# Hash matmuls in two column halves, PSUM copies moved to ScalarE, a first head without DMAs between its operands, and a new order: one core of Trainium2

## The chip, the core and the metric

The kernel runs on one core of one Trainium2 chip. A core has TensorE (PE in the profile; its weight loads are shown as PEld), VectorE (DVE), ScalarE (ACT), GpSimd (POOL) and SyncE (SP, which only issues DMAs here). Matmul results land in PSUM, from where VectorE or ScalarE must copy them to SBUF. The metric is the device time of one execution in microseconds.

## The reference

Sixteen attention heads (batch 2, 8 heads, 768 positions, width 64) whose mask is a hash: a query sees a key only if the signs of their projections on 6 vectors agree. Then two layers over 1536 tokens of width 512 with 2048 hidden units each.

```python
q_bits = (np.einsum('bhsd,dk->bhsk', q, proj) > 0)
k_bits = (np.einsum('bhsd,dk->bhsk', k, proj) > 0)
...
mask = q_bucket[:, :, :, None] == k_bucket[:, :, None, :]
scores = scale * np.matmul(q, k.transpose(0, 1, 3, 2))
scores = np.where(mask, scores, -1000000000.0)
scores = scores - np.max(scores, axis=-1, keepdims=True)
attn = np.exp(scores)
attn = attn / (np.sum(attn, axis=-1, keepdims=True) + 1e-09)
return np.matmul(attn, v).astype(np.float32)
...
h = x @ w_in                                   # layer 0
g = np.maximum(h, 0.0) + np.log1p(np.exp(-np.abs(h)))
return (g @ w_out).astype(np.float32)
...
h = x @ w_in                                   # layer 1
relu6 = np.clip(h + 3.0, 0.0, 6.0)
g = h * relu6 / 6.0
return (g @ w_out).astype(np.float32)
```

The weights of the layers come as 64-bit floats.

## The kernel before

**No loop of the program sets the order of the work.** Every step is entered in a plan (`Schedule.add`) with its engine or engines, an assumed cost in microseconds, what it reads and writes, and a priority (a due time). `Schedule.run` (line 98) then plays the plan through with those costs: at each step it takes, on the unit that comes free first, the ready operation with the least due time, gives an operation that two engines may do to the one that ends it first, and writes it out. The emitted order on each engine is fixed and in order. So a change of a cost or of a due time (`TH`, `WHEN`, `STEP`, `PROJECT`, `ACTIVATE`, `FETCH`, `AHEAD`, lines 35 to 48) moves operations on all engines.

**A head** (`prepare`, line 279, and `attend`, line 375). Three loads bring `raw` (keys transposed in partitions 0 to 63, queries in 64 to 127, in two DMAs) and `rawk` (the keys twice). Scores are taken with split numbers: `qa` holds the rest and the rounded part of the queries, `ka` the rounded keys twice, `qb` the rounded queries again and `kb` the rest of the keys; rows 64 to 95 of `qb` and `kb` hold the hash bits, which add a large positive number where query and key agree. The bits come from the hash matmuls `dot` (line 339): `hashes` times `raw`, one matmul for each half of the 768 positions, both summed into all 128 rows of the PSUM tile `d`. A comparison on VectorE (L356) turns `d` into `bt`, and four DMAs (L365) send `bt` to the rows of `qb` and `kb`. One more DMA (L334) copies the rounded queries from `qa` to `qb`.

For each of 6 query tiles: four score matmuls into `sc` (L392, L393; two PSUM buffers), the row maximum (`nm`, L406, VectorE) and a bias (`bs`, L413, VectorE), the exponential (`e`, L421, ScalarE), six transposes into `tp` (L432, one PSUM buffer), and a copy of `tp` to `et` in SBUF (`even`, L436, by either engine). Per head: 12 value matmuls into `av` (L448; each pair writes rows 0 to 63 and 64 to 127 of the same tile; a matmul in full precision, as these and the hash matmuls are, shows as two rows of the trace), a copy to `xa` (by either engine), three transposes into `pt`, the reciprocal of the row sums (`rec`, two VectorE instructions, L474 and L478), and a scaled copy to `xn` (L485). Per two heads, transposes `xt` and a split into `xh` and `xl`.

**Layers.** Weights are loaded as 64-bit words and converted by seven operations per tile (`convert`: two on ScalarE, five on VectorE, all on tiles called `raw`, `bits`, `w`). Each layer has 32 tiles. The first 12 of layer 0 have room beside the attention; its other 20 wait until the attention's SBUF is free, and those of layer 1 until the tiles of layer 0 that lie in their place have had their last use, in the third group. Hidden matmuls `ph` (L605, 12 for each of 16 blocks in 3 groups of 512 tokens), then the activation, then projections into `acc` (L697 in layer 0, L699 in layer 1, 12 for each block). The activation of layer 0 goes ScalarE (`me`, `mu`, `ml`), VectorE (`me`, L665), GpSimd (`ml`, L672, shown as L231), VectorE (`ml`, L676), ScalarE (`gh`), VectorE (`gl`).

Copies, casts and subtractions are recorded at the lines of their helpers: L226 is a copy on ScalarE, L228 a copy on VectorE, L231 a subtraction on VectorE or GpSimd; the tile names tell them apart.

## Time and profile before

| | us |
|---|---|
| median of 3 runs (843.8 to 844.47) | 844.27 |
| the profiled execution's own time | 844.39 |
| its span, first to last instruction | 842.7 |
| TensorE busy | 799.3 (95%) |
| VectorE busy | 558.9 (66%) |
| ScalarE busy | 451.5 (54%) |
| GpSimd busy | 92.1 (11%) |

What lies outside the span is 1.7 us. The granted TensorE clock is 1.00 of full speed (2.4 GHz) in every stretch, which says nothing of matmuls at the very start: the first ones take about twice as long as later ones of their kind.

A row of the page's groups reads: line, engine, operation, output<-input, shapes, count | busy time, mean ns of one | idle time of the engine before them and what ended it. A row of the order of time reads: start, duration, engine, line, operation, and in brackets the idle time before it with its releaser. Durations overlap a little: an instruction often starts some 0.07 to 0.1 us before the one ahead of it has ended, so the distance of two starts is the cost on a full engine. A busy TensorE is not TensorE at its peak, since ends of matmuls are modelled. The program falls into an opening (no exponential yet), the sixteen heads, and the two layers.

### The profile page before, as it was taken

What the parts mean: (1) busy time and instruction counts of PE and PEld (TensorE: products, weight loads), DVE (VectorE), ACT (ScalarE), POOL (GpSimd) and SP (SyncE); (2) the same over time, 40 slices, a digit from 0 to 9 for tenths busy, and PEclk for the clock granted to TensorE, in tenths of its full rate; (3) what the DMA queues carried; (4) which work ended last, traced back from release to release, by engine and by line L of the source; (5) the groups of instructions that cost most, each with busy time, mean ns of one, the idle gap of its engine ahead of it and who ended that gap; (6) DMA issues with size and microseconds to landing.
All of it is one profiled execution on the core that took longest, in us unless ns stands there. A gap on an engine that the chain in (4) does not pass through costs nothing.

```text
span 842.7 us, 10395 instructions
## 1 busy us (share of the span) xinstructions
PE 799.3 (95%) x3808; PEld 604.5 (72%) x3808; DVE 558.9 (66%) x958; ACT 451.5 (54%) x764; POOL 92.1 (11%) x85
## 2 busy tenths in 40 slices
PE   4899999999999999999999999999999999999997
PEld 2666666666666667677888776677888888888886
DVE  4989999999887889964333698989942322232222
ACT  1677677777665767656554766775532322232222
POOL 1000000000000242322222224340000000000000
PEclk9999999999999999999999999999999999999999
DMA  7584323332310650000000255451000100010001
GB/s 191 166 271 103 82 80 93 86 85 75 86 29 28 254 228 0 1 1 1 0 1 1 93 157 167 158 175 50 1 1 1 50 1 1 0 51 1 1 0 51
DMA packets 26771, 59.40 MB, mean 70 GB/s; under 512 B 3680, under 2 KB 7776, under 8 KB 26720
## 3 DMA queue, kind: packets, MB, share of 16 engines
q1 hardware_dynamic: 24224, 52.45, 20.6%
q10 hardware_dynamic: 2496, 6.29, 2.1%
q8 instruction: 30, 0.49, 0.2%
q14 instruction: 21, 0.17, 0.1%
HBM read 49.29 MB, written 3.15 MB: 62 GB/s over the span
## 4 chain that ended last, share of the span: by engine, by line
PE 65%; DVE 16%; ACT 5%; DMA 5%; POOL 4%; issue 4%; SPq 1%; ACTq 0%; DVEq 0%; POOLq 0%
PE ph L605 22%; PE acc L699 16%; PE acc L697 7%; PE av L448 7%; PE tp L432 5%; POOL ml L231 4%; PE sc L392 4%; PE sc L393 3%; DVE gl L231 2%; DVE bits L576 2%; DVE bits L569 2%; PE d L340 2%; ACT e L421 2%; DMA raw<-in_moe_w_out_dram 2%; DVE me L665 2%
## 5 line engine op out<-in xcount | busy, mean ns | idle before, releaser
L605 PE MATMUL ph<-xh,w 128*128 128x512 f32 x768 | 240.8, 395 | 0.8 <-ACT xa L226 0.6
L605 PEld LDWEIGHTS ph<-xh,w 128*128 128x128 f32 x768 | 143.7, 188 | 34.5 <-ACT xa L226 1.3
L605 PE MATMUL ph<-xl,w 128*128 128x512 f32 x384 | 151.2, 394 | 0.0
L421 ACT ACTIVATE e<-sc,bs 128x768 f32<-128x768 f32 x96 | 95.0, 990 | 64.2 <-DVE bs L413 44.9
L634 DVE SCALAR_TENSOR_TENSOR ml<-me,ph 128x512 f32<-128x512 f32 x48 | 33.0, 687 | 124.6 <-ACT me L629 124.6
L697 PE MATMUL acc<-gh,w 128*128 128x512 f32 x384 | 101.0, 400 | 11.7 <-ACT gh L226 11.3
L231 POOL TENSOR_TENSOR ml<-ml,me 128x512 f32<-128x512 f32 x48 | 85.9, 1789 | 210.3 <-DVE me L665 154.2
L406 DVE TENSOR_REDUCE nm<-sc 128x1 f32<-128x768 f32 x96 | 91.7, 955 | 22.1 <-PE sc L393 20.6
L629 ACT ACTIVATE me<-ph,three 128x512 f32<-128x512 f32 x48 | 33.1, 689 | 133.7 <-PE ph L605 130.7
L699 PE MATMUL acc<-w,gh 128*128 128x512 f32 x384 | 97.8, 393 | 0.0
L697 PEld LDWEIGHTS acc<-gh,w 128*128 128x128 f32 x384 | 69.9, 188 | 37.2 <-ACT gh L226 22.7
L605 PEld LDWEIGHTS ph<-xl,w 128*128 128x128 f32 x384 | 72.1, 188 | 17.0
L699 PEld LDWEIGHTS acc<-w,gh 128*128 128x128 f32 x384 | 72.1, 188 | 16.7
L392 PE MATMUL sc<-ka,qa 128*128 128x384 f32 x192 | 76.7, 400 | 7.0 <-ACT e L421 6.6
L432 PE MATMUL tp<-ident,e 128*128 128x128 f32 x576 | 80.1, 275 | 3.2 <-DVE et L228 1.7
L432 PEld LDWEIGHTS tp<-ident,e 128*128 128x128 f32 x576 | 66.8, 140 | 16.0 <-ACT et L226 5.2
L448 PE MATMUL av<-et,vx 128*64 128x384 f32 x384 | 72.1, 498 | 0.0
L393 PE MATMUL sc<-kb,qb 96*128 96x384 f32 x192 | 66.1, 344 | 2.3 <-DMA kb<-bt 2.3
L392 PEld LDWEIGHTS sc<-ka,qa 128*128 128x128 f32 x192 | 36.8, 192 | 38.6 <-ACT e L421 15.5
L676 DVE SCALAR_TENSOR_TENSOR ml<-ph,ml 128x512 f32<-128x512 f32 x48 | 33.0, 687 | 38.7 <-POOL ml L231 38.7
L697 PE MATMUL acc<-gl,w 128*128 128x512 f32 x192 | 54.4, 397 | 2.8 <-ACT xh L226 2.1
L231 DVE TENSOR_TENSOR gl<-ml,gh 128x512 fp32r<-128x512 f32 x48 | 38.5, 801 | 26.0 <-ACT gh L226 26.0
(62 smaller groups left out, 1030.4 us busy)
## 6 DMA issues: line engine op xcount, KB each, us to landing
raw<-in_moe_w_in_dram SPq DMA_DIRECT2D x26, 512.0 KB, 4.6
raw<-in_moe_w_out_dram SPq DMA_DIRECT2D x26, 512.0 KB, 3.5
rawk<-in_kv_dram SPq DMA_DIRECT2D x16, 384.0 KB, 4.2
raw<-in_kv_dram SPq DMA_DIRECT2D x16, 192.0 KB, 3.2
raw<-in_q_dram SPq DMA_DIRECT2D x16, 192.0 KB, 3.4
vx<-in_kv_dram SPq DMA_DIRECT2D x16, 192.0 KB, 2.4
qb<-qa SPq DMA_DIRECT2D x16, 192.0 KB, 4.1
raw<-in_moe_w_in_dram ACTq DMA_DIRECT2D x6, 512.0 KB, 8.8
```

The lines of the kernel that those rows point to most:

```text
L231: engines[e].tensor_tensor(out, a, b, op=ALU.subtract)
L392: nc.tensor.matmul(o, qa[h].ap[:, qs], ka[h].ap[:, cs], start=True, stop=False)
L393: nc.tensor.matmul(o, qb[h].ap[0:KB, qs], kb[h].ap[0:KB, cs], start=False, stop=True)
L406: lambda e, sc=sc, t=t: nc.vector.reduce_max(nm.ap[:, t, 0:1], sc.ap[:, :, :HALF], axis=AX.XY, negate=True),
L421: lambda e, sc=sc, ex=ex, t=t: nc.scalar.activation(ex.ap.rearrange("p (u k) -> p u k", u=2), sc.ap[:, :, :HALF], AF.Exp, bias=bs.ap[:, t, ...
L432: nc.tensor.transpose(o, ex.ap[:, c * P : (c + 1) * P], ident.ap)
L448: nc.tensor.matmul(av.ap[u * D : (u + 1) * D, :HALF], vx[h].ap[:, c, :], et[u].ap[:, c, :], start=(c == 0), stop=(c == NT - 1),)
L605: nc.tensor.matmul(bank(), w[:, a, :], x[b].ap[:, kc, :], start=(kc + i == 0), stop=(kc == KC - 1 and i == 2))
L629: dict(A=0.478), lambda e: nc.scalar.activation(e1.ap, bank(), AF.Relu, bias=three.ap),
L634: lambda e: nc.vector.scalar_tensor_tensor(l.ap, e1.ap, 6.0, bank(), op0=ALU.min, op1=ALU.mult),
L697: nc.tensor.matmul(o, w.ap[:, a, cs], b.ap, start=st, stop=sp)
L699: nc.tensor.matmul(o, b.ap[:, cs], w.ap[:, a, :], start=st, stop=sp)
```

## The change

- **Hash matmuls.** `hashes` shrinks from 192 to 64 columns. The two halves no longer sum into one another: each is a matmul with 64 output rows, the first into rows 0 to 63 of `d`, the second into rows 64 to 127.
- **ScalarE.** Of the six copies `et` of a head, those with t = 1, 2, 4, 5 may go to ScalarE alone, the other two to either engine. `xa`, and from the second head on `ka` and the rounded queries in `qa`, go to ScalarE alone.
- **GpSimd.** The first of the two `rec` instructions moves from VectorE to GpSimd.
- **First head.** It has no `rawk` load: both halves of `ka` are made from `raw`, one by each engine. `qb`'s queries are a ScalarE copy, and the bits are written to `qb` and `kb` by four VectorE comparisons on 32 rows each. `raw` is loaded first and `proj` after it, its second half issued by ScalarE.
- **The plan.** All due times and several costs are new, among them GpSimd's subtraction (1.3 to 1.8), and the plan adds 0.09 where TensorE goes from one kind of matmul (full array, column halves, transposes) to another.

```diff
-TH = 11.573
-WHEN = dict(load_p=-28.21, load_k=-19.20, load_q=-23.34, ...
+TH = 10.375
+WHEN = dict(load_p=-19.19, load_k=-19.20, load_q=-16.41, ...
...
+SWITCH = 0.09
...
+                        if e == "T" and op.mode != mode:
+                            end += SWITCH
...
-    for s0 in (0, D):
-        plan.add(
-            dict(S=0.625), lambda e, s0=s0: nc.sync.dma_start(out=p32.ap[s0 : s0 + D, :], in_=proj),
+    for s0, e in ((0, "S"), (D, "A")):
+        plan.add(
+            {e: 0.625 if e == "S" else 0.06}, lambda e, s0=s0: engines[e].dma_start(out=p32.ap[s0 : s0 + D, :], in_=proj),
...
-    hashes = buffer("heads", [P, 6 * ROWS], F32, "hash", 1, "hash")
+    hashes = buffer("heads", [P, 2 * ROWS], F32, "hash", 1, "hash")
...
-        wide, narrow = dict(A=0.74, D=0.48), dict(D=0.88)
+        wide, narrow = dict(A=0.74) if h else dict(A=0.74, D=0.48), dict(D=0.88)
...
+            for s0, e in ((0, "D"), (D, "A")):
+                plan.add(
+                    {e: wide[e]}, lambda e, s0=s0: cast(e, ka[h].ap[s0 : s0 + D, :], raw.ap[0:D, :]),
...
+            plan.add(
+                dict(A=0.74), lambda e: cast(e, qb[h].ap[0:D, :], f32(qa[h].ap[D:P, :])),
...
-        def dot(u):
-            nc.tensor.matmul(
-                dots.ap[:, :HALF], hashes.ap[:, (1 - u) * 2 * ROWS : (3 - u) * 2 * ROWS],
-                raw.ap[:, u * HALF : (u + 1) * HALF], start=(u == 0), stop=(u == 1),
-            )
...
+        def dot(e):
+            for u in range(2):
+                nc.tensor.matmul(
+                    dots.ap[u * D : (u + 1) * D, :HALF], hashes.ap, raw.ap[:, u * HALF : (u + 1) * HALF],
+                    start=True, stop=True,
+                )
...
+        if h == 0:
+            for u in range(2):
+                for n, x in enumerate((qb, kb)):
+                    rows = slice((2 * u + n) * ROWS, (2 * u + n + 1) * ROWS)
+                    plan.add(
+                        dict(D=0.5),
+                        lambda e, u=u, x=x, rows=rows: nc.vector.tensor_scalar(
+                            x[h].ap[D:KB, u * HALF : (u + 1) * HALF], dots.ap[rows, :HALF], thr.ap[rows, 0:1],
+                            top.ap[rows, 0:1], op0=ALU.is_gt, op1=ALU.mult,
+                        ),
...
-                dict(A=0.81, D=0.95), even, reads=[tp], writes=[et[t // n]], prio=step + WHEN["even"],
+                dict(A=0.73) if t % 3 else dict(A=0.73, D=0.88), even, reads=[tp], writes=[et[t // n]], prio=step + WHEN["even"],
...
-            dict(A=0.49, D=0.46), lambda e: cast(e, xa.ap, av.ap[:, :HALF]),
+            dict(A=0.44), lambda e: cast(e, xa.ap, av.ap[:, :HALF]),
...
-            dict(D=0.08), lambda e: nc.vector.tensor_scalar(rec.ap, den.ap, 1e-9, None, op0=ALU.add),
+            dict(P=0.3), lambda e: nc.gpsimd.tensor_scalar(rec.ap, den.ap, 1e-9, None, op0=ALU.add),
...
-            dict(P=1.3), lambda e: minus(e, l.ap, l.ap, e1.ap), reads=[l, e1], writes=[l], prio=prio
+            dict(P=1.8), lambda e: minus(e, l.ap, l.ap, e1.ap), reads=[l, e1], writes=[l], prio=prio
```

Numbers of lines from the change on are up to 27 higher in the new kernel. How the emitted order moves is shown at three places.

VectorE from the program's start (behind a memset) to the first row maximum `nm0_0`, before (numbers behind a name are the head's, then the query tile's):

```order
L272 TENSOR_SCALAR hash_113<-p32_98 64x6 x4
L228 CAST ka0_125<-rawk0_103 128x768
L315 TENSOR_SCALAR qa0_128<-raw0_110 64x768
L231 TENSOR_TENSOR kb0_136<-raw0_110,ka0_125 64x768
L320 SCALAR_TENSOR_TENSOR qa0_128<-raw0_110,qa0_128 64x768
L356 TENSOR_SCALAR bt0_146<-d0_134,thr_78,top_79 128x384
L315 TENSOR_SCALAR qa1_148<-raw1_123 64x768
L231 TENSOR_TENSOR kb1_153<-raw1_123,ka1_138 64x768
L320 SCALAR_TENSOR_TENSOR qa1_148<-raw1_123,qa1_148 64x768
L356 TENSOR_SCALAR bt1_161<-d1_155,thr_78,top_79 128x384
L406 TENSOR_REDUCE nm0_76<-sc0_0_169 128x1
```

And after:

```order
L233 CAST ka0_117<-raw0_100 64x768
L321 TENSOR_SCALAR qa0_120<-raw0_100 64x768
L277 TENSOR_SCALAR hash_76<-p32_105 64x6 x4
L326 SCALAR_TENSOR_TENSOR qa0_120<-raw0_100,qa0_120 64x768
L236 TENSOR_TENSOR kb0_137<-raw0_100,ka0_117 64x768
L373 TENSOR_SCALAR qb0_139<-d0_134,thr_80,top_81 32x384
L373 TENSOR_SCALAR kb0_137<-d0_134,thr_80,top_81 32x384
L373 TENSOR_SCALAR qb0_139<-d0_134,thr_80,top_81 32x384
L373 TENSOR_SCALAR kb0_137<-d0_134,thr_80,top_81 32x384
L326 SCALAR_TENSOR_TENSOR qa1_144<-raw1_115,qa1_144 64x768
L236 TENSOR_TENSOR kb1_160<-raw1_115,ka1_149 64x768
L433 TENSOR_REDUCE nm0_78<-sc0_0_155 128x1
```

One cast from `rawk0` is replaced by one from `raw0`, four writes of bits stand in the place of `bt0`, and head 1's `bt1` no longer stands ahead of the first maximum.

ScalarE around the exponentials of head 10, before (`et` are copies of transposed scores, `bits` and `w` parts of a weight conversion, `ka`, `qa`, `xa`, `xh` copies of other heads):

```order
L421 ACTIVATE e10_0_1875,den10_1876<-sc10_0_1830,bs10_1854 128x768
L226 ACTIVATE et9_1_1837<-tp9_5_1883 128x6x128
L421 ACTIVATE e10_1_1913,den10_1876<-sc10_1_1867,bs10_1854 128x768
L421 ACTIVATE e10_2_1940,den10_1876<-sc10_2_1894,bs10_1854 128x768
L226 ACTIVATE et10_0_1923<-tp10_1_1933 128x6x128
L552 ACTIVATE bits0_2_3_1957<-raw0_2_3_522 128x512
L421 ACTIVATE e10_3_1967,den10_1876<-sc10_3_1927,bs10_1854 128x768
L226 ACTIVATE w0_2_1_1974<-bits0_2_1_1592 128x512
L226 ACTIVATE xa9_1980<-av9_1918 128x384
L421 ACTIVATE e10_4_2001,den10_1876<-sc10_4_1950,bs10_1854 128x768
L226 ACTIVATE et10_1_2006<-tp10_3_1987 128x6x128
L313 ACTIVATE qa12_2022<-raw12_1769 64x768
```

And after:

```order
L448 ACTIVATE e10_0_1877,den10_1878<-sc10_0_1818,bs10_1854 128x768
L231 ACTIVATE et9_1_1869<-tp9_4_1880 128x6x128
L448 ACTIVATE e10_1_1910,den10_1878<-sc10_1_1865,bs10_1854 128x768
L231 ACTIVATE et9_1_1869<-tp9_5_1901 128x6x128
L448 ACTIVATE e10_2_1933,den10_1878<-sc10_2_1894,bs10_1854 128x768
L448 ACTIVATE e10_3_1953,den10_1878<-sc10_3_1915,bs10_1854 128x768
L231 ACTIVATE et10_0_1937<-tp10_1_1955 128x6x128
L448 ACTIVATE e10_4_1972,den10_1878<-sc10_4_1947,bs10_1854 128x768
L231 ACTIVATE ka12_1981<-rawk12_1669 128x768
L319 ACTIVATE qa12_1992<-raw12_1713 64x768
L231 ACTIVATE et10_0_1937<-tp10_2_1984 128x6x128
L448 ACTIVATE e10_5_2014,den10_1878<-sc10_5_1969,bs10_1854 128x768
```

The weight conversions are gone from here, and a copy `et` follows most exponentials. Over the whole program ScalarE makes 73 of the 96 copies `et` where it made 46, and all 16 copies `xa` where it made 5.

VectorE in the third group of layer 0, from the operand `me` that GpSimd waits for to the operation `ml` that waits for GpSimd, before:

```order
L665 SCALAR_TENSOR_TENSOR me0_2_2_4447<-mu0_2_2_4459,me0_2_2_4447 128x512
L231 TENSOR_TENSOR gl0_2_1_4475<-ml0_2_1_4422,gh0_2_1_4467 128x512
L576 SCALAR_TENSOR_TENSOR bits1_0_1_4430<-raw1_0_1_4396,bits1_0_1_4430 128x512
L557 TENSOR_SCALAR bits1_0_2_4485<-bits1_0_2_4485 128x512
L562 TENSOR_SCALAR bits1_0_2_4485<-bits1_0_2_4485 128x512
L676 SCALAR_TENSOR_TENSOR ml0_2_2_4473<-ph0_2_2_4391,ml0_2_2_4473 128x512
```

And after:

```order
L692 SCALAR_TENSOR_TENSOR me0_2_2_4423<-mu0_2_2_4441,me0_2_2_4423 128x512
L236 TENSOR_TENSOR gl0_2_1_4453<-ml0_2_1_4401,gh0_2_1_4444 128x512
L589 TENSOR_SCALAR bits1_0_1_4416<-bits1_0_1_4416 128x512
L596 SCALAR_TENSOR_TENSOR bits1_0_0_4413<-raw1_0_0_4352,bits1_0_0_4413 128x512
L596 SCALAR_TENSOR_TENSOR bits1_0_1_4416<-raw1_0_1_4371,bits1_0_1_4416 128x512
L603 SCALAR_TENSOR_TENSOR bits1_0_0_4413<-raw1_0_0_4352,bits1_0_0_4413 128x512
L703 SCALAR_TENSOR_TENSOR ml0_2_2_4451<-ph0_2_2_4390,ml0_2_2_4451 128x512
```

Between the two stand four operations before, two of them the short kind of one input, and five after, three of them of the long kind.

## Rows read from the trace of the kernel before

**Rows 1.** The page's head: the span.

```profile
span 842.7 us, 10395 instructions
```

**Rows 2.** Busy time by stretch (start:end, length, engines, clock, DMA share, GB/s).

```profile
31.90:145.90 114.00, 108.29 (x650) 74.15 (x649) 105.39 (x195) 81.25 (x140) 1.57 (x7) 1.00 0.48 140
145.90:273.00 127.10, 122.92 (x744) 84.53 (x743) 113.16 (x208) 84.56 (x147) 2.15 (x7) 1.00 0.25 65
273.00:365.00 92.00, 85.69 (x370) 63.10 (x370) 83.78 (x144) 64.08 (x112) 28.30 (x13) 1.00 0.31 114
470.00:580.00 110.00, 101.25 (x416) 76.06 (x415) 99.33 (x167) 77.75 (x134) 33.08 (x16) 1.00 0.48 153
580.00:842.00 262.00, 257.79 (x1117) 209.22 (x1115) 94.98 (x153) 76.66 (x119) 0.00 (x0) 1.00 0.04 13
```

**Rows 3.** The start of the program in order of time, all engines.

```profile
0.80 1.23 SPq L263 DMA_DIRECT2D p<-in_proj_dram  x2
...
2.07 0.59 SPq L299 DMA_DIRECT2D rawk<-in_kv_dram  x1
...
5.46 0.56 DVE L228 CAST ka<-rawk 128x768 fp32r<-128x768 f32 x1 [1.44 <-DMA rawk<-in_kv_dram]
...
7.74 2.90 PE L340 MATMUL d<-raw,hash 128*128 128x384 f32 x4 [7.74 <-DMA raw<-in_q_dram]
...
9.20 0.95 DVE L320 SCALAR_TENSOR_TENSOR qa<-raw,qa 64x768 fp32r<-64x768 f32 x1
9.48 0.84 ACT L226 ACTIVATE ka<-rawk 128x768 fp32r<-128x768 f32 x1 [7.40 <-DMA rawk<-in_kv_dram]
...
10.75 0.68 DVE L356 TENSOR_SCALAR bt<-d,thr,top 128x384 fp32r<-128x384 f32 x1 [0.60 <-PE d L340]
...
17.90 0.66 PE L393 MATMUL sc<-kb,qb 96*128 96x384 f32 x1 [2.33 <-DMA kb<-bt]
...
20.49 0.99 ACT L421 ACTIVATE e<-sc,bs 128x768 f32<-128x768 f32 x1 [10.16 <-PE sc L393]
...
26.50 0.81 ACT L226 ACTIVATE et<-tp 128x768 f32<-128x768 f32 x1 [0.23 <-PE tp L432]
...
27.21 0.99 ACT L421 ACTIVATE e<-sc,bs 128x768 f32<-128x768 f32 x1
```

**Rows 4.** Matmuls in order of time, two places in the heads.

```profile
155.24 0.33 PE L393 MATMUL sc<-kb,qb 96*128 96x384 f32 x1
155.50 1.51 PE L448 MATMUL av<-et,vx 128*64 128x384 f32 x8
156.94 0.88 PE L432 MATMUL tp<-ident,e 128*128 128x128 f32 x6
...
179.77 0.33 PE L393 MATMUL sc<-kb,qb 96*128 96x384 f32 x1
179.95 1.50 PE L340 MATMUL d<-raw,hash 128*128 128x384 f32 x4
181.28 0.82 PE L432 MATMUL tp<-ident,e 128*128 128x128 f32 x6
```

**Rows 5.** Groups by line, whole span (busy us, mean ns | idle before, releaser).

```profile
L228 DVE COPY et<-tp 128x768 f32<-128x768 f32 x50 | 47.3, 946 | 2.0 <-PE tp L432 2.0
L228 DVE COPY xa<-av 128x384 f32<-128x384 f32 x11 | 6.1, 558 | 2.7 <-PE av L448 2.2
L569 DVE SCALAR_TENSOR_TENSOR bits<-raw,bits 128x512 int32<-128x512 int32 x64 | 45.5, 717 | 0.2
```

**Rows 6.** Waits from 40 to 280 us: waiter <- releaser, us in total, times, longest.

```profile
ACT e L421 <- DVE bs L413: 42.6, 46, 2.1
ACT et L226 <- PE tp L432: 13.9, 18, 1.6
```

**Rows 7.** Waits from 285 to 365 us.

```profile
DVE ml L676 <- POOL ml L231: 5.4, 5, 1.2
```

**Rows 8.** Waits from 470 to 580 us.

```profile
DVE ml L676 <- POOL ml L231: 7.2, 6, 1.2
```

More of the change, by code (lines that the diff above doesn't have):

```diff
@@ L124, in run @@
                 tick = int(start / TICK)
-                busy[tick] = busy.get(tick, 0.0) + op.cost[e] * op.duty
+                busy[tick] = busy.get(tick, 0.0) + op.cost[e]
+                mode = op.mode
             free[e] = op.done
@@ L297, in prepare @@
         )
-        plan.add(
-            first, lambda e: engines[e].dma_start(out=rawk.ap, in_=kv[head][:, :S]),
-            writes=[rawk], prio=at + WHEN["load_q"], dma=1.1,
-        )
+        if h:
+            rawk = buffer("heads", [P, S], F32, "rawk", 2, f"rawk{h}")
+            plan.add(
+                first, lambda e: engines[e].dma_start(out=rawk.ap, in_=kv[head][:, :S]),
+                writes=[rawk], prio=at + WHEN["load_q"], dma=1.1,
+            )
         plan.add(
@@ L345, in prepare @@
-        last = ()
-        for u in range(2):
-            last = [
-                plan.add(
-                    dict(T=0.66), lambda e, u=u: dot(u),
-                    reads=[raw, hashes], writes=[dots], prio=at + WHEN["dots"], after=last,
-                )
-            ]
+        if h:
+            plan.add(
+                queue, lambda e: engines[e].dma_start(out=f32(qb[h].ap[0:D, :]), in_=f32(qa[h].ap[D:P, :])),
+                reads=[qa[h]], writes=[qb[h]], prio=at + WHEN["copy_q"], dma=0.55,
+            )
+        else:
+            plan.add(
+                dict(A=0.74), lambda e: cast(e, qb[h].ap[0:D, :], f32(qa[h].ap[D:P, :])),
+                reads=[qa[h]], writes=[qb[h]], prio=at + WHEN["high_q"],
+            )
```

64 lines of the change are left out of this document (33 added, 31 removed).

## The prediction

> **What bounds the kernel now.** I read the span first [rows 1], then the busy time by stretch [rows 2], then the opening in order of time [rows 3], then the waits [rows 6 to 8]. The execution took 844.39 us, of which 842.7 lie in the span; the median of the runs shown is 844.27, so nothing has to be scaled. The stretches are cut at the starts of the last exponentials of heads 0, 7 and 15. In heads 1 to 7 (114.0 us, 16.3 a head) VectorE is busy 105.4 us, ScalarE only 81.2, and TensorE 108.3, though its ends are modelled. In heads 8 to 15 (127.1 us, 15.9 a head) it is 113.2, 84.6 and 122.9. So two engines are nearly full there and the third has a quarter to a third of its time free: ScalarE's exponentials waited 42.6 us for the bias that VectorE makes [rows 6]. Behind the heads come two stretches in which weight conversions fill VectorE (83.8 of 92.0 us and 99.3 of 110.0), and between and after them TensorE works without a gap (257.8 of 262.0, which has the end of the run in it) [rows 2]. There nothing is to be had: all 2304 layer matmuls stay. Before the heads lies an opening: the first exponential starts at 20.49 us [rows 3].
>
> **The opening.** The chain there is: load, hash matmuls, bits, four DMAs of bits, first scores. The score matmul that waited longest for bits ran at 17.90, while `bt0` had started at 10.75 [rows 3]. After the change the loads of `raw0` are SyncE's first, at 0.80 where `proj` was; 384 KB took from 2.07 to 5.46 to land, 3.4 us, so the second half, issued some 0.6 later, lands about 0.80 + 0.6 + 3.4 = 4.8. `proj` follows and lands within the same time. Hash scalings take some 0.6 more (5.5). The matmuls at the start took 2.90 us, and half of that, 1.45, if the two halves run at once (7.0). VectorE meanwhile makes the two remainders, each 0.95 [rows 3], until about 7.5, then four comparisons at the price of `bt`, 0.68 each: 10.2. The last score matmuls of the first tile end by 10.9. The order puts head 1's two remainders ahead of the first maximum: 1.9 more, 12.1 to 12.2; they need `rawk1`, which took from its issue 5.6 us to come and started its cast at 9.48 [rows 3], in the new order hardly later. Maximum and bias bring the first exponential to about 13.4, 7 us earlier. The ramp of head 0 gains another 1 us, since its three later pairs of hash matmuls, which stand between the first tiles, are halved too. I take **8 us**; bounds 5 (head 1's loads come 2 us late and hold the maxima behind them) and 9.5 (they cost nothing).
>
> **TensorE's part of a head.** The hash matmuls took 1.33 us (179.95 to 181.28). A pair of column halves is in the trace: `av`, four matmuls in two pairs, took 1.44 (155.50 to 156.94) [rows 4]. So a pair costs 0.72 with its share of going in and out. Entering it costs 0.26 from the last score matmul's start where the hash matmuls now cost 0.18: 0.08 more, and leaving it as much, of which the 0.72 holds half [rows 4]. 0.72 + 0.04 + 0.08 = 0.84, a saving of **0.5 us a head**; bounds 0.3 and 0.64. The Trainium skill (TensorEngine Tiling (Array Packing), Key Properties) says that a change of tiling mode drains TensorE, and that tiles of one mode run in parallel; the rows agree, with 0.08 for a change. By its factor of up to 2 alone the saving would be 0.67 a head, some 3 us more in all; nothing else here rests on that.
>
> **VectorE against ScalarE.** The emitted order says who does what. In heads 1 to 7 VectorE makes 5 copies `et` instead of 21 and none of 5 `xa`, while ScalarE makes 36 instead of 21. All 12 early weight tiles are now converted by head 7 (VectorE 60 operations of theirs there instead of 36); in heads 8 to 15 there were 24 and are none. A copy `et` costs VectorE 0.946 and `xa` 0.558 [rows 5], ScalarE 0.81 for `et`, and on a full engine the next starts 0.1 earlier (26.50 to 27.21 [rows 3]), so I take 0.87, 0.47 and 0.72. A conversion operation of the long kind is 0.717 [rows 5], 0.62 on a full engine; the short kind is about half.
> Heads 1 to 7, VectorE: 16 x 0.87 + 5 x 0.47 + small ones 2.1 = 18.4 off; 16 x 0.62 + 8 x 0.34 for the conversions = 12.6 on. Sum 105.4 - 5.8 = 99.6. ScalarE: 15 x 0.72 + casts and `xa` 3.3 + nine conversion operations at some 0.55 (512 columns, where `et` has 768) 4.9 = 19.0 on: 100.2. TensorE: five hash pairs, 108.3 - 2.5 = 105.8.
> Heads 8 to 15, VectorE: 9 x 0.87 + 6 x 0.47 + conversions 12.6 + small ones 4.7 = 27.9 off: 85.3. ScalarE: 9 x 0.72 + 6.4 - 4.9 = 8.0 on: 92.6. TensorE: seven pairs, 122.9 - 3.5 = 119.4.
> So in the early heads all three engines end near 100 to 106 of busy time, and what waits on what is open. At the share that VectorE had (105.4 of 114.0) its 99.6 would need 108; with three engines in one ring I take 110: **4 us** off, bounds -3 and 8. In the late heads only TensorE is left near full: at its present share 119.4 needs 123.5, and VectorE's relief ends part of the waits that its modelled ends hide: 121, **6 us** off, bounds 3 and 9.
> The `rec` instruction on GpSimd and the six fewer DMAs of head 0 lie beside other work: GpSimd is busy 2 us of 127 in the heads [rows 2], and the reciprocal behind it on VectorE comes after other work. I cost them at nothing; a late `rec` would hold VectorE's next maximum, at most some tenths a head.
>
> **The layers.** The order of the conversions is new, their number is not. In the third group VectorE has five operations between the one that feeds GpSimd and the one that waits for it, where it had four; counted at the prices above that is about 0.35 us more cover for each block, and it holds for most blocks of the first group too. VectorE waited there 5 times for 5.4 us and 6 times for 7.2 [rows 7, 8]; 0.4 off each of 11 is 4 us, at most the 12.6. Against it, more conversions stand ahead of the first block's `gl`, so the first projection starts later; the stretch is VectorE's, whose sum stays, so that costs at most its idle time at the start. I take **3 us** off, bounds -4 and 10.
>
> **The sum.** 8 + 4 + 6 + 3 = 21 off 844.39: 823.4, against the median 823. With every term at its bound it is 5 - 3 + 3 - 4 = 1 off at one end and 9.5 + 8 + 9 + 10 = 36 at the other.
>
> **The rivals.**
> *Only the opening pays.* Three engines of equal load wait for one another, or the hash halves don't run at once (the change then does not do what it says in its first line: 0.16 a head more instead of 0.5 less). For it: TensorE was already busy 97% of the late heads [rows 2]. Against it: 42.6 us of exponentials waiting for VectorE [rows 6]. 844.4 - 8 - 2 = 834.
> *All waits for VectorE vanish.* The heads fall to TensorE's own work and GpSimd's latency is covered: 9.5 + 8 + 9 + 10 = 36 off: 808.
> *ScalarE holds the ring: slower.* Its queue is in order, and a copy `et` must wait for its transposes; behind it stand exponentials for which transposes and, through the two score buffers, TensorE wait. Of the 45 ScalarE copies between 40 and 280 us, 18 waited, 13.9 us in all, up to 1.6 [rows 6]. ScalarE's free time in heads 1 to 15 was 241.1 - 165.8 = 75 us [rows 2], of which 27 are filled, leaving 48; with the 8 of the opening there are 56 for waits of its 69 copies there. It decides from a mean wait of 0.81 us on every copy, against 0.31 now. At a mean of 1.0 the result is 844.4 + 69 - 56 = 857.
> *Nothing moves.* Head 1's loads or bits eat the opening's gain and the heads stay: 843 to 846.
>
> **How the numbers follow.** Forecast 0.62, with its own range 813 to 830; only the opening 0.17; all waits vanish 0.11; ScalarE slower 0.06; nothing moves 0.04. A measurement of this kernel tells about 0.2%, or 1.7 us, from no change: faster 0.90, same 0.04, slower 0.06. The range goes from 809, which takes in a part of the best case, to 838, which takes in the opening-only case: about 8 in 10.
>
> **What would show it.** The first exponential near 13.4 us instead of 20.49. Hash pairs of about 0.75 us. Heads 8 to 15 near 15.1 us each with VectorE at about 70% and ScalarE 77% busy; heads 1 to 7 near 15.7 with both above 88%. From the last exponential to the end 566 to 570 us instead of 569.7 (273.0 to 842.7). VectorE's waits for GpSimd in the conversion stretches under 9 us. I would be wrong if copies `et` on ScalarE wait about a microsecond each, if the heads keep 16 us though VectorE is idle, or if TensorE waits more than now at the start of the layers.

## The result, and the profile after

The changed kernel takes **830.04 us** (median of 4 runs, 829.67 to 832.18), the kernel before in the same comparison 844.03 us (4 runs, 843.19 to 844.47). The ratio is 0.984, 95% interval 0.982 to 0.986: 1.6% faster. The profiled execution took 829.67 us, its span is 827.9. All lines of the page and the trace are up to 27 higher than before.

Cut where the prediction cut, at the starts of the last exponentials of heads 0, 7 and 15 (27.24, 134.69 and 254.49 us; before 31.89, 145.93 and 273.04):

| us | before | after | difference |
|---|---|---|---|
| start to first exponential | 20.49 | 14.31 | -6.2 |
| ramp of head 0, from its first to its last exponential | 11.40 | 12.93 | +1.5 |
| heads 1 to 7 | 114.0 | 107.4 | -6.6 |
| heads 8 to 15 | 127.1 | 119.8 | -7.3 |
| last exponential to the end of the span | 569.7 | 573.4 | +3.7 |
| span | 842.7 | 827.9 | -14.8 |

The two stretches of the heads in the kernel after, from the answer to [rows 2] (start:end, length, busy time and count of PE, PEld, DVE, ACT and POOL, granted clock, DMA share, GB/s):

```profile
27.20:134.70 107.50, 102.99 (x636) 69.84 (x636) 99.71 (x188) 99.16 (x170) 4.36 (x15) 1.00 0.50 148
134.70:254.50 119.80, 118.45 (x744) 81.09 (x742) 87.43 (x155) 91.29 (x158) 3.88 (x15) 1.00 0.25 69
```

In heads 8 to 15 VectorE is now busy 87.4 us instead of 113.2 and ScalarE 91.3 instead of 84.6; TensorE, 118.5 of 119.8, has hardly a gap left. That it sets the pace there is borne out below by the run with full hash matmuls. In heads 1 to 7 all three have 99 to 103 of 107.5.

The opening after in order of time, the answer to [rows 3] (start, duration, engine, line, operation, idle time before it and its releaser):

```profile
6.32 1.55 PE L361 MATMUL d<-raw,hash 128*64 128x384 f32 x4 [6.32 <-DVE hash L277]
7.28 0.95 DVE L236 TENSOR_TENSOR kb<-raw,ka 64x768 fp32r<-64x768 f32 x1
8.26 0.67 DVE L373 TENSOR_SCALAR qb<-d,thr,top 32x384 fp32r<-32x384 f32 x1
10.37 0.69 DVE L373 TENSOR_SCALAR kb<-d,thr,top 32x384 fp32r<-32x384 f32 x1
12.08 0.95 DVE L236 TENSOR_TENSOR kb<-raw,ka 64x768 fp32r<-64x768 f32 x1
13.06 0.96 DVE L433 TENSOR_REDUCE nm<-sc 128x1 f32<-128x768 f32 x1
14.31 0.99 ACT L448 ACTIVATE e<-sc,bs 128x768 f32<-128x768 f32 x1 [4.98 <-DVE bs L440]
16.57 0.52 PE L420 MATMUL sc<-kb,qb 96*128 96x384 f32 x1
16.89 1.48 PE L459 MATMUL tp<-ident,e 128*128 128x128 f32 x6
19.54 0.99 ACT L448 ACTIVATE e<-sc,bs 128x768 f32<-128x768 f32 x1 [3.08 <-DVE bs L440]
20.84 0.87 PE L459 MATMUL tp<-ident,e 128*128 128x128 f32 x6
22.09 0.33 PE L420 MATMUL sc<-kb,qb 96*128 96x384 f32 x1
```

Up to the maximum at 13.06 it went as reckoned, VectorE's queue with hardly a gap. Then come six transposes in 1.48 us and scores in 0.52, where the same shapes take 0.87 and 0.33 from 20.8 us on. The ramp of before ran mostly after that moment, the ramp of after mostly ahead of it.

The waits in heads 1 to 15 after, the answer to [rows 6] (waiter, released by: us in total, times, longest):

```profile
DVE nm L433 <- PE sc L420: 28.4, 30, 1.9
ACT e L448 <- DVE bs L440: 16.3, 23, 1.7
ACT et L231 <- PE tp L459: 14.3, 21, 1.9
```

And in heads 1 to 15 of the kernel before, where [rows 6] has other bounds:

```profile
ACT e L421 <- DVE bs L413: 44.5, 46, 2.2
DVE nm L406 <- PE sc L393: 16.9, 36, 1.3
PE sc L392 <- ACT e L421: 5.7, 12, 0.8
```

Exponentials waited 44.5 us for VectorE before and wait 16.3 now. The copies on ScalarE wait for transposes about as much as before (13.9), though there are many more of them. VectorE's wait for scores rose from 16.9 to 28.4 us. The last row will matter below: score matmuls wait for ScalarE's exponentials, which must free one of the two score buffers; after the change it is 3.9 us.

### The profile page after: what moved, and what is told of

It reads as the page before. It is cut to its first block, busy times and chain, and to the rows that moved or that the text cites. A ratio compares the mean times of both kernels' runs of the same rounds, so it can differ in the third digit from the quotient of the medians.

```text
span 827.9 us, 10408 instructions
## 1 busy us (share of the span) xinstructions
PE 791.3 (96%) x3808; PEld 595.6 (72%) x3808; DVE 525.4 (63%) x899; ACT 481.4 (58%) x812; POOL 93.5 (11%) x101
## 4 chain that ended last, share of the span: by engine, by line
PE 70%; DVE 15%; ACT 5%; issue 3%; POOL 3%; DMA 2%; POOLq 0%; SPq 0%; ACTq 0%; DVEq 0%
PE ph L632 23%; PE acc L726 16%; PE acc L724 9%; PE av L475 7%; PE tp L459 6%; PE sc L419 4%; PE sc L420 3%; POOL ml L236 3%; DVE gl L236 2%; DVE bits L603 2%; DMA raw<-in_moe_w_out_dram 2%; DVE bits L596 1%; DVE w L236 1%; DVE me L692 1%; DVE bits L589 1%
## 5 line engine op out<-in xcount | busy, mean ns | idle before, releaser
L656 ACT ACTIVATE me<-ph,three 128x512 f32<-128x512 f32 x48 | 33.1, 689 | 130.0 <-PE ph L632 126.9
L236 POOL TENSOR_TENSOR ml<-ml,me 128x512 f32<-128x512 f32 x48 | 82.6, 1722 | 217.4 <-DVE me L692 137.3
L632 PEld LDWEIGHTS ph<-xl,w 128*128 128x128 f32 x384 | 72.1, 188 | 16.9
L231 ACT ACTIVATE et<-tp 128x768 f32<-128x768 f32 x73 | 59.1, 809 | 17.0 <-PE tp L459 16.2
L679 ACT ACTIVATE me<-ph 128x512 f32<-128x512 f32 x48 | 28.4, 592 | 53.7 <-PE ph L632 52.8
```

The lines of the kernel that those rows point to most:

```text
L231: nc.scalar.activation(out, in_, AF.Copy)
L236: engines[e].tensor_tensor(out, a, b, op=ALU.subtract)
L632: nc.tensor.matmul(bank(), w[:, a, :], x[b].ap[:, kc, :], start=(kc + i == 0), stop=(kc == KC - 1 and i == 2))
L656: dict(A=0.478), lambda e: nc.scalar.activation(e1.ap, bank(), AF.Relu, bias=three.ap),
```

## The experiments

All ratios are to the kernel before, run on the same chip. Stages are read from the starts of exponentials as above. "Due times" are `TH` and `WHEN`; "rules" are the engine rules for `et`, `xa`, `ka`, `qa` and `rec`. A plan with another rule, cost or due time is played through anew, so the order of other things moves too; four runs keep the order to the row, which is said. Stages are those of one profiled execution, which can lie off the median: by 2.5 us for "before, rules", and by 1.8 for "after without rules", where the granted clock was 0.98 in heads 1 to 7.

| us (profiled run) | first exp. | ramp | heads 1-7 | heads 8-15 | rest | ratio, interval |
|---|---|---|---|---|---|---|
| before | 20.5 | 11.4 | 114.0 | 127.1 | 569.7 | 1 |
| after | 14.3 | 12.9 | 107.4 | 119.8 | 573.4 | 0.984 (0.982-0.986) |
| after, full hash, same order | 15.3 | 11.2 | 110.4 | 121.9 | 573.2 | 0.987 (0.986-0.988) |
| after without rules | 14.6 | 13.3 | 113.5 | 126.6 | 572.6 | 0.995 (0.994-0.997) |
| after with old due times | 15.5 | 11.8 | 112.4 | 124.8 | 571.5 | 0.992 (0.991-0.993) |
| before, hash halves, same order | 20.4 | 11.7 | 114.2 | 126.9 | 569.6 | 1.001 (1.000-1.002) |
| before, new first head | 18.8 | 11.3 | 114.6 | 126.8 | 569.1 | 0.996 (0.995-0.998) |
| before, rules | 21.5 | 12.4 | 115.5 | 128.5 | 572.2 | 1.005 (1.003-1.007) |
| before, due times | 18.1 | 12.7 | 113.5 | 125.5 | 574.0 | 1.002 (1.001-1.003) |
| before, rules and due times | 19.4 | 11.9 | 114.5 | 126.5 | 573.9 | 1.004 (1.002-1.005) |
| after, zeros ahead, same order | 14.3 | 13.1 | 107.7 | 119.8 | 573.2 | 0.982 (0.981-0.984) |
| after, zeros in the gaps, same order | 14.3 | 10.7 | 108.1 | 119.8 | 573.4 | 0.980 (0.979-0.982) |
| after, GpSimd cost 1.3 | 14.1 | 13.0 | 108.2 | 119.8 | 573.7 | 0.982 (0.981-0.983) |
| after, zeros and GpSimd cost by group | 14.3 | 10.7 | 108.3 | 119.8 | 569.8 | 0.977 (0.976-0.978) |

### What the hash halves are worth: two runs with the order kept

```diff
-                    dots.ap[u * D : (u + 1) * D, :HALF], hashes.ap, raw.ap[:, u * HALF : (u + 1) * HALF],
-                    start=True, stop=True,
+                    dots.ap[:, :HALF], hashes.ap[:, (1 - u) * 2 * ROWS : (3 - u) * 2 * ROWS],
+                    raw.ap[:, u * HALF : (u + 1) * HALF], start=(u == 0), stop=(u == 1),
```

> The changed kernel with the same emitted order on every engine, but the hash matmuls of all heads written as before: all 128 output rows twice, the second half summed onto the first. My theory: TensorE sets the pace in heads 8 to 15 (busy 118.5 of 119.8 us there), so each full hash costs the 0.5 us that I reckoned for a pair's saving, in 8 heads surely and in heads 1 to 7 mostly: 830.0 + 4 to 8 = 834 to 838, with the late heads 4 us longer than 119.8. Rival: the heads wait in a ring of three engines and TensorE has slack that its modelled ends hide; then the time moves by less than 2 us, 830 to 832, and the hash halves were not what gave the late heads their gain.

Measured: 833.5 us, 2.4 to 3.5 us above the changed kernel (by the ratio and by the medians). The first theory's 834 to 838 is just missed. Its sign held, its size did not: the late heads took 121.9 instead of 119.8 us, so 2.1 where 4 were expected, for seven hash sets 0.29 each. The rows show where it goes. First the kernel after, then the one with full hash matmuls, the same place of a head (columns as in the opening):

```profile
199.61 0.87 PE L459 MATMUL tp<-ident,e 128*128 128x128 f32 x6
200.42 0.87 PE L361 MATMUL d<-raw,hash 128*64 128x384 f32 x4
201.21 0.44 PE L419 MATMUL sc<-ka,qa 128*128 128x384 f32 x1
201.49 0.34 PE L420 MATMUL sc<-kb,qb 96*128 96x384 f32 x1
```

```profile
203.06 0.87 PE L459 MATMUL tp<-ident,e 128*128 128x128 f32 x6
203.77 1.46 PE L361 MATMUL d<-raw,hash 128*128 128x384 f32 x4
204.77 0.63 PE L419 MATMUL sc<-ka,qa 128*128 128x384 f32 x1
205.24 0.34 PE L420 MATMUL sc<-kb,qb 96*128 96x384 f32 x1
```

From the transposes' start to the second score it is 1.88 us with halves and 2.18 with full matmuls: 0.30. Going in costs 0.10 more with halves (0.81 against 0.71 from `tp` to `d`), and from `d` to the second score it is 1.07 against 1.47, 0.40 less. In heads 1 to 7, where three engines are near full, five full sets cost 3.0 us, 0.6 each. Some of that is not theirs: this run's ramp was 1.7 us shorter than the changed kernel's, for a reason shown below, and in the run with zeros in the gaps a ramp 2.3 us shorter went with heads 1 to 7 longer by 0.6. Why the rest is more than 0.30 a set is not shown.

The other run is the kernel before in its own order, with the hash matmuls alone in halves (the diff above the other way).

> The kernel before in its own order on every engine, with the hash matmuls alone written as two column halves. With the changed kernel the full form cost 0.3 us a head more than the halves. My theory: in the kernel before VectorE sets the pace, so little of these 16 x 0.3 = 4.8 us comes through; up to 1.5 us in the late heads: 842.5 to 844.3. Rival: TensorE's part is on the path of every head there too: 839.5 to 840.

Measured: 845.9 against 845.0, ratio 1.001. The time is above both ranges, but so is the kernel before in this comparison (845.0). Nothing came through, which fits the theory of a kernel whose pace VectorE sets. The same edit is worth about 3 us in one kernel and none in the other.

### Rules and due times: neither pays alone, nor both

```diff
-        wide, narrow = dict(A=0.74) if h else dict(A=0.74, D=0.48), dict(D=0.88)
+        wide, narrow = dict(A=0.74, D=0.48), dict(D=0.88)
...
-                dict(A=0.73) if t % 3 else dict(A=0.73, D=0.88), even, ...
+                dict(A=0.73, D=0.88), even, ...
...
-            dict(A=0.44), lambda e: cast(e, xa.ap, av.ap[:, :HALF]),
+            dict(A=0.44, D=0.46), lambda e: cast(e, xa.ap, av.ap[:, :HALF]),
...
-            dict(P=0.3), lambda e: nc.gpsimd.tensor_scalar(rec.ap, den.ap, 1e-9, None, op0=ALU.add),
+            dict(D=0.08), lambda e: nc.vector.tensor_scalar(rec.ap, den.ap, 1e-9, None, op0=ALU.add),
```

> The changed kernel, due times and hash halves and first head as they are, with the ScalarE-only rules taken back: et, xa, ka and the rounded queries may go to either engine, rec's first step is on VectorE. The plan is played through anew: VectorE then makes 62 of the 96 copies et instead of 23. My theory: the copies moved to ScalarE gave heads 1 to 7 their 6.5 us, since VectorE sets the pace there; with them back on VectorE these heads are 114 us again and the late heads a little longer: 836 to 840. Rival: hash halves and new due times gave the gain, and the planner's choice of engine does not matter while the sum of the three engines stays: 829 to 832.

Measured: 840.5 us, just above the theory's upper end, heads 1 to 7 at 113.5. Its two stretches of heads, and their main wait:

```profile
27.80:141.30 113.50, 103.68 (x630) 70.22 (x630) 105.00 (x194) 80.28 (x140) 1.45 (x7) 0.98 0.49 142
141.30:267.90 126.60, 122.54 (x756) 82.08 (x752) 117.08 (x214) 78.62 (x140) 1.16 (x7) 1.00 0.24 66
```

```profile
ACT e L448 <- DVE bs L440: 42.8, 45, 1.9
```

VectorE is full again (105.0 and 117.1) and exponentials wait 42.8 us for it, as in the kernel before. So the rules are needed in this kernel. Are they enough? The kernel before with the rules alone:

> The kernel before with the new rules on engines alone (four of six copies et, xa, and ka and the rounded queries from the second head on by ScalarE alone, rec's first step on GpSimd), due times as before, the plan played through anew: ScalarE then makes 79 copies et instead of 46. Without these rules the changed kernel gave back all that its heads 1 to 15 had gained (240.1 us instead of 227.3, before 241.1). My theory: they carry the gain also by themselves: 15 heads x 0.5 to 0.8 us, 832 to 837. Rival one: without due times made for them the copies wait in ScalarE's queue and most is lost: 839 to 844. Rival two, the slower one of the prediction: ScalarE holds the ring, above 846.

Measured: 849.4, slower than before; the theory fell, and the time is that of the third case, rival two. Is it by its mechanism? Heads 1 to 15 of this run (stretch, then waits):

```profile
33.90:277.90 244.00, 230.10 (x1391) 157.91 (x1390) 184.46 (x339) 196.60 (x334) 7.74 (x29) 1.00 0.38 100
```

```profile
DVE nm L406 <- PE sc L393: 51.3, 45, 3.4
ACT et L226 <- PE tp L432: 19.0, 27, 1.4
ACT e L421 <- DVE bs L413: 15.5, 23, 1.6
PE sc L392 <- ACT e L421: 10.2, 14, 1.2
```

VectorE's busy time fell from 218.5 to 184.5 us as meant, and the wait for its bias from 44.5 to 15.5. In their place VectorE waits 51.3 us for score matmuls (16.9 before), and TensorE is idle for 13.9 us (9.9 before). Most of that idle time ends with an exponential on ScalarE: score matmuls wait 10.2 us for one, before 5.7. This is the path that the prediction named for its ScalarE rival, through the two score buffers. But ScalarE's copies wait 19.0 us in all (13.9 before), far from the 0.81 us on each at which the prediction had that rival begin, and ScalarE is busy 196.6 of 244.0 us. So the third case came out by its number and in part by its path; what share of the loss is ScalarE's queue, and what share the place of the scores in TensorE's order, no run separates. With VectorE out of the way, the scores do not come early enough in the old order. Do they with the new due times? Three runs:

```diff
-TH = 11.573
-WHEN = dict(load_p=-28.21, load_k=-19.20, load_q=-23.34, ...
+TH = 10.375
+WHEN = dict(load_p=-28.21, load_k=-19.20, load_q=-16.41, ...
```

> The kernel before with the new due times of the heads alone (the one for the load of proj left as it was); engines may be chosen as before, hash matmuls and first head as before. One corner of four, with the new rules on engines alone (heads 1 to 15 took 244.0 us, before 241.1) and both together. My theory: due times and rules need each other. VectorE is nearly full as long as it makes half of the copies, so the new order alone gives little: heads 1 to 15 in 238 to 242, the whole within 841 to 846. Rival: the due times carry the gain alone: heads 1 to 15 in 233 or less, 837 or less.

> The kernel before with the new due times and the new rules on engines, without the hash halves and the new first head. The changed kernel's heads 1 to 15 took 227.3 us, with full hash matmuls 232.2. My theory: rules and due times together carry what the heads gained beyond the hash halves: heads 1 to 15 in 231 to 234, the whole 836 to 839. Rival: the gain hangs on the hash halves or the earlier start as well: heads above 237, 841 or more.

> The changed kernel with the due times of the heads of before (but proj loaded behind raw): rules on engines, hash halves and first head as changed. My theory: with the old due times the scores come late on TensorE, as with the rules alone, where VectorE waited 51.3 us for scores in heads 1 to 15 against 28.4 in the changed kernel; heads 1 to 15 take 236 to 241 us and the whole 837 to 843. Rival: hash halves and the corrected costs of the plan make up for it, heads 1 to 15 in 227 to 231, 829 to 832.

Measured: due times alone 846.6 (heads 1 to 15 239.0 us), rules and due times 847.8 (240.9), and the changed kernel with the old due times 837.7 (237.2). The first came within its range for the heads (the whole is 0.6 above), the third as expected; the second did not: its rival held. In that run VectorE still waits for scores:

```profile
DVE nm L406 <- PE sc L393: 42.8, 49, 4.1
ACT et L226 <- PE tp L432: 21.5, 27, 1.9
```

In the changed kernel that wait is 28.4, with full hash matmuls in its order 27.9, with the old due times 48.0. So in the changed kernel the due times do bring the scores earlier, and their return costs heads 1 to 15 10.0 us; on the kernel before with the rules they bring that wait only from 51.3 to 42.8. Between this run (heads 240.9) and the one with full hash matmuls (232.3) lie the new first head, the plan's corrected costs (the change of matmul kind, the maximum, the exponential and others), and that the order was planned for hash halves, in one step for each head. The first head alone moves heads 1 to 15 by nothing (241.4, below). By difference the costs, those of the hash step among them, would be worth some 8 us, given rules and due times; no run changes them alone, so this is inferred and not shown.

### The first head alone

The edit is that of the change to `prepare` for `h == 0` and to the load of `proj`, on the kernel before.

> The kernel before with the new first head alone (no rawk load for it, casts from raw, a ScalarE copy and four comparisons instead of five DMAs, raw loaded first); all other due times, rules and the full hash matmuls as before, the plan played through anew. My theory: what the opening gains stays to the end, since the heads run back to back behind it: the last exponential of head 0 comes some 4 to 6 us earlier than 31.89, and the whole takes 838.5 to 840.5. Rival: VectorE has no less work in all, so the heads 1 to 7, which it bounds, take back what the opening gives: 842.5 to 844.5, with heads 1 to 7 some 4 us longer than 114.0.

Measured: 842.2 against 845.0, ratio 0.996 (0.995 to 0.998). The last exponential of head 0 came at 30.1 instead of 31.9 us and heads 1 to 15 took 241.4: what the opening gained went to the end, as the theory says, but it gained 1.8 us and not 4 to 6, so the whole misses the theory's range. The rival fell: heads 1 to 7 took 0.5 us more and not 4, heads 8 to 15 0.3 less. Neither the old due times alone nor the full hash matmuls alone held the opening back: the changed kernel has its last exponential of head 0 at 27.2 us with those, at 26.6 with these. Which other part of the change brings the opening's remaining 2.8 us is not shown.

### Why the ramp of head 0 became longer: zeros for TensorE

```diff
+    zero = buffer("heads", [P, 512], BF16, "zero", 1, "zero")
+    spare = buffer("ps", [P, 512], F32, "av", 1, "spare")
+    def idle_work(e, n):
+        for i in range(n):
+            nc.tensor.matmul(spare.ap, zero.ap[:, :P], zero.ap, start=True, stop=True)
+    plan.add(dict(T=0.0), lambda e: idle_work(e, 12), reads=[zero], writes=[spare], prio=-50, mode=None)
```

> The changed kernel in the same order, with 12 matmuls of zeros (128x128 by 128x512, 16-bit) put ahead of the first hash matmuls on TensorE, which had nothing to do until 6.3 us. Their results are not used. My theory for the opening's smaller gain (4.7 us up to the last exponential of head 0 instead of 8): until some 20 us every matmul takes twice its later time, though the granted clock shows 1.00, and after the change the ramp of head 0 falls into that time, which the ramp of before did only half. With TensorE kept busy from 1 to 6 us the score matmuls of head 0 come in single time, its last exponential starts 2 to 3 us earlier (24.5 to 25.2 instead of 27.2) and the whole takes 827 to 828. Rival one: VectorE sets the ramp, which then gets at most 0.7 us shorter: 829.3 to 830. Rival two: such matmuls change nothing in how long the later ones take: 830, or slower by what the zeros delay.

Measured: 829.9 us, the ramp 13.1. The theory's time fell and both rivals' held, but neither says quite what the rows show (stretches of the opening, columns as above, and two scores):

```profile
6.00:9.00 3.00, 2.01 (x7) 0.48 (x5) 2.86 (x6) 0.90 (x2) 0.00 (x0) 1.00 0.94 292
9.00:12.00 3.00, 1.54 (x5) 1.24 (x6) 2.89 (x4) 1.12 (x2) 0.00 (x0) 0.76 0.88 220
12.00:15.00 3.00, 2.51 (x8) 0.81 (x6) 2.92 (x4) 0.75 (x1) 0.00 (x0) 0.50 0.55 168
18.00:21.00 3.00, 3.00 (x11) 1.47 (x10) 2.02 (x4) 1.08 (x2) 0.00 (x0) 0.54 0.16 35
```

```profile
9.97 0.34 PE L429 MATMUL sc<-ka,qa 128*128 128x384 f32 x1
12.51 0.52 PE L430 MATMUL sc<-kb,qb 96*128 96x384 f32 x1
```

Behind the zeros the first scores did take 0.34 to 0.44 us. In that time TensorE had nothing to do for 1.7 and then for 0.7 us, the granted clock fell to 0.50, which is 1.2 GHz, and the scores took 0.52 as in the changed kernel. So the gaps were filled too:

```diff
             nc.tensor.matmul(o, qa[h].ap[:, qs], ka[h].ap[:, cs], start=True, stop=False)
+            if h == t == 0:
+                idle_work(e, 3 if u else 7)
...
+            if h == 1:
+                idle_work(e, 11)
```

> The changed kernel in the same order, with the 12 zero matmuls ahead of the first hash matmuls and 21 more in TensorE's gaps behind them (7 and 3 among the scores of the first query tile, 11 behind the second hash matmuls); nothing of them is used. With the first 12 alone the hash matmuls took 1.17 instead of 1.55 us and the first scores single time, but TensorE then had nothing to do for 1.7 and 0.7 us, the granted clock went from 1.00 to 0.76 and 0.50, and the ramp stayed as it was (27.3). My theory: the double time of the matmuls is what makes the ramp long; with the gaps filled they keep single time to the end of the ramp, the last exponential of head 0 starts at 25 to 25.5 instead of 27.2, and the whole takes 827.5 to 828.5. Rival: VectorE's queue sets the ramp (copies and maxima in turn), at most 0.7 us come off: 829.3 to 830.

Measured: 827.95 us, the ramp 10.7. Two stretches of its opening, and three instructions in order of time:

```profile
9.00:12.00 3.00, 2.46 (x12) 1.34 (x10) 2.88 (x4) 0.71 (x1) 0.00 (x0) 1.00 0.90 255
12.00:15.00 3.00, 3.00 (x16) 1.19 (x15) 2.92 (x4) 0.75 (x1) 0.00 (x0) 1.00 0.56 183
```

```profile
16.02 0.34 PE L434 MATMUL sc<-kb,qb 96*128 96x384 f32 x1
16.20 0.82 PE L473 MATMUL tp<-ident,e 128*128 128x128 f32 x6
...
24.90 0.99 ACT L462 ACTIVATE e<-sc,bs 128x768 f32<-128x768 f32 x1 [0.33 <-DVE bs L454]
```

The clock stays at 1.00, scores take 0.34, and the last exponential of head 0 starts at 24.90 instead of 27.24. This settles the cause of the longer ramp: in the same order it is 2.3 us shorter with TensorE at full speed, and the run with the first 12 zeros alone, whose clock fell again, gained nothing. Head 1 gave some 0.4 us back; the span fell by 1.7. The run with full hash matmuls says the same without zeros: its second hash set kept TensorE at work until 16 us, its scores took 0.34 from 16.75 on, and its ramp was 11.2.

### The part behind the heads: one number of the plan

```diff
-            dict(P=1.8), lambda e: minus(e, l.ap, l.ap, e1.ap), reads=[l, e1], writes=[l], prio=prio
+            dict(P=1.3), lambda e: minus(e, l.ap, l.ap, e1.ap), reads=[l, e1], writes=[l], prio=prio
```

The order stays the same to the row if `STEP`, `PROJECT`, `ACTIVATE`, `FETCH` and `AHEAD` are set back as well: of these numbers, GpSimd's cost alone moves the layers' order.

> The changed kernel with one number of the plan as before: GpSimd's subtraction at 1.3 instead of 1.8. The order of the heads stays the same, that of the layers changes: the copy gh stands right behind the next block's absolute value on ScalarE again, ahead of the exponential, and the conversions lie otherwise among the activations. My theory: of the 3.7 us that the part behind the last exponential became longer, the 1.3 us of 12 waits for gh of 0.27 us and some of the later start of the blocks of the first group come from this number: 827 to 828.7. Rival: the loss is attention work of TensorE that moved behind the last exponential (about 2.6 us) and the rest noise of the order: within 1 us of 830.

Measured: 829.8, by the ratio and by the stages (rest 573.7) no different from the changed kernel, as the rival said. Read by token group, from the start of the last exponential or of the last `gl` of the group ahead ("by group" is the last run below):

| us | before | after | cost 1.3 | by group |
|---|---|---|---|---|
| first group | 107.2 | 112.3 | 111.1 | 110.2 |
| second | 89.8 | 90.3 | 89.8 | 89.8 |
| third, to the `gl` of layer 1's third block | 115.7 | 114.0 | 115.6 | 111.5 |
| from there to the end | 257.0 | 256.8 | 257.2 | 258.4 |

The wait that the theory named is there in the kernel after and gone in this run, but the whole gained nothing by it. In the second group of the kernel after, in order of time, and its wait:

```profile
426.90 0.60 ACT L679 ACTIVATE me<-ph 128x512 f32<-128x512 f32 x1 [2.70 <-PE ph L632]
427.53 0.63 ACT L683 ACTIVATE me<-me 128x512 f32<-128x512 f32 x1
428.07 0.61 ACT L231 ACTIVATE gh<-ml 128x512 fp32r<-128x512 f32 x1
```

```profile
PEld acc L724 <- ACT gh L231: 3.3, 12, 0.3
```

`gh` stands behind the exponential, TensorE's weight load waits for it twelve times 0.27 us, and a block takes 5.67 us instead of 5.55. With 1.3 that wait is gone and a block takes 5.55 again. (The granted clock was 0.98 in the first group of that run, which may be the 1.0 us between the table's last two columns, equal in cost there.) But 1.8 had gained 1.5 us in the third group, which 1.3 loses. The first group stays long either way, and much of that is moved work. From the last exponential to the start of the group's last `gl`, after and before:

```profile
254.50:366.80 112.30, 103.68 (x457) 77.51 (x453) 89.52 (x155) 75.65 (x133) 31.45 (x17) 1.00 0.26 94
273.00:380.20 107.20, 100.89 (x436) 75.52 (x436) 91.66 (x155) 72.64 (x127) 32.17 (x16) 1.00 0.26 98
```

TensorE is busy 2.8 us more there, with 18 transposes `tp` behind the mark instead of 12 and 30 rows of `av` instead of 24. So some 2.8 of the 7.3 us that heads 8 to 15 gained were only put behind the mark.

Both numbers are right somewhere. GpSimd's subtractions in the kernel after: 12 from the second group, then two from the first, which took 3.16 and 1.62 us (busy us, mean ns):

```profile
L236 POOL TENSOR_TENSOR ml<-ml,me 128x512 f32<-128x512 f32 x12 | 15.5, 1292 | 55.3 <-DVE me L692 55.3
L236 POOL TENSOR_TENSOR ml<-ml,me 128x512 f32<-128x512 f32 x2 | 4.8, 2388 | 6.6 <-ACT w L231 4.2 <-ACT me L679 2.4
```

Hence the last run: zeros, and the cost by group.

```diff
-            dict(P=1.8), lambda e: minus(e, l.ap, l.ap, e1.ap), reads=[l, e1], writes=[l], prio=prio
+            dict(P=1.8 if g == 2 else 1.3), lambda e: minus(e, l.ap, l.ap, e1.ap), reads=[l, e1], writes=[l], prio=prio
```

> The changed kernel with the 33 zero matmuls in the opening (their results are not used) and with GpSimd's subtraction planned at 1.3 in the first two groups of tokens and at 1.8 in the third. With the zeros the span was 826.2. With 1.3 in all groups the first group took 111.2 instead of 112.3 us, the second 89.7 instead of 90.2, the third 1.5 more. My theory: the two gains stay and the loss goes, 1.0 to 1.6 us: the whole 826.2 to 827.2. Rival: where the cost changes between groups the order shifts and takes the gain back: 827.7 to 829.

Measured: **825.46 us**, ratio 0.977 (0.976 to 0.978), faster than both kernels, its interval apart from that of the changed kernel. The span is 822.8, the rest 569.8. It is more than I expected. Against the kernel after, the first group is 2.1 us shorter and the second 0.5. The third took 111.5 us where 114.0 was the best so far, but layer 1 then took 1.6 longer: TensorE is busy 105.0 us in the third group and 106.3 in the kernel after, so about half of the 2.5 us is work moved behind the mark, and 1.0 us stays to the end. The order of the third group is new, and no run takes it apart.

## Why the prediction was right, and where its terms were not

The forecast was 823 within 809 to 838; 830 lies within, and at the very end of the 813 to 830 given for the likeliest case. That case came true in its outline, with four terms of other sizes. Of 21 us forecast 14 came by the medians, 14.8 between the two spans that the stages add up to. The opening gave 3.4 us less than its term, the layers 6.7 less, the heads 3.9 more, of which 2.8 were only moved into the layers' part. That 830 is inside owes more to the width of the range than to the terms.

- **Opening: 8 us forecast (5 to 9.5), 4.65 measured.** The first exponential was right but for 0.9 us (14.31 for 13.4), nearly all of it there when the comparisons began (8.26 for 7.5, VectorE's own queue); the comparisons of 0.67 to 0.69 us and the two remainders of head 1 ahead of the maximum came as reckoned. Wrong was the step "The ramp of head 0 gains another 1 us": it lost 1.5. I had put down in the profile section that the first matmuls take twice as long, used that for the hash matmuls, and forgot that a ramp which starts 6 us earlier lies in that time. The run with zeros in the gaps shows that this was worth 2.3 us.
- **TensorE's part of a head: 0.5 us forecast (0.3 to 0.64), 0.29 to 0.30 measured** in the late heads with the order kept. The low bound was the value. Going in costs 0.10 more in the rows (0.08 reckoned). The mis-sized term is what follows: a pair of 0.72 for 1.33, with 0.04 for going out, was to bring 0.57, and the rows show 0.40 for both together, which they do not part. The 0.67 that the prediction worked out from the factor of up to 2 is shown by no run.
- **Heads 1 to 7: 4 us forecast, 6.6 measured.** Busy times were as reckoned, 99.7 for VectorE (99.6) and 99.2 for ScalarE (100.2); TensorE's 103.0 is 2.8 below its 105.8. The guess was how well three equal engines mesh: 107.4 and not 110.
- **Heads 8 to 15: 6 us forecast, 7.3 measured, some 2.8 of it only moved** behind the last exponential. VectorE 73% (70 forecast), ScalarE 76% (77), 14.98 us a head (15.1): right. TensorE sets the pace, as the full-hash run shows by 2.1 us of longer late heads.
- **Layers: 3 us off forecast (-4 to 10), 3.7 on measured.** The failed step is "0.4 off each of 11": VectorE's waits for GpSimd were to be under 9 us and are 12.2, before 12.6. One more operation of cover in the order was not one more in time; why the wait kept its length is not shown:

```profile
DVE ml L703 <- POOL ml L236: 7.4, 6, 1.5
DVE ml L703 <- POOL ml L236: 4.8, 4, 1.2
```

  (the first in 254.5 to 350, the second in 457 to 567 us, the answers to [rows 7, 8]). What I had left out is that a cut at the last exponential does not hold TensorE's unfinished attention work fast, 2.8 us here.
- **ScalarE holds the ring: fell.** The copies waited 14.3 us in 21 places, far from 0.81 us on each of 69. The rules on the kernel before did make it slower, 1.005; there VectorE waits for scores, and scores wait for ScalarE's exponentials (10.2 us, 5.7 before), which is part of this rival's path without its size.
- **Only the opening pays: fell**, though nearer than I thought: no single part of the change that was run, nor rules with due times, shortens the heads of before by more than 2.2 us. What I took as a sum of terms, each from its own rows, works together. Taken back one at a time from the changed kernel, the rules cost heads 1 to 15 12.9 us, the due times 10.0 and the hash halves 5.0, together twice the 13.9 that these heads gained in all.

## What to carry to other kernels

When a full engine is relieved, ask in which order the next one gets its work: here 34 us less on VectorE were worth nothing or less on the kernel before, with its old due times or with the new ones, and the same rules carried 12.9 us of the heads in the changed kernel, where scores came earlier. A saving on an engine counts only while that engine sets the pace (0.30 us a head in one kernel, none in the other). When an opening is shortened, ask how fast TensorE runs when the work now begins: 33 matmuls of zeros in its idle places gave 2.3 us of ramp. And when stages are compared, ask what moved across the mark between them.
